# Attention and two MoE layers on one core: block 0 and block 1 scaled by pairs of heads, the third weight unit loaded and decoded sooner, other idle products

## The chip, the cores and the metric

The kernel runs on one core of a Trainium2 chip. Its engines are TensorE (PE, with PEld for its weight loads), VectorE (DVE), ScalarE (ACT), GpSimd (POOL) and SyncE (SP, which here only issues DMAs). The metric is the device time of one execution in microseconds; the median of three runs of the kernel before is 1569.9 us (1569.37 to 1571.35).

## The reference

```
kv  = k^T v per batch and head          (8 batches, 8 heads, 576 rows, head size 64)
out = q kv
x   = out / rms(out over a head) * g_norm            -> 4608 rows of 512
xn  = x / rms(x over 512) * rms_g
h   = silu(xn @ w_gate) * (xn @ w_val)                (512 x 1536 each)
x2  = h @ w_out                                       (1536 x 512)
y   = relu(x2 @ w_in)^2 @ w_out2                      (512 x 2048, 2048 x 512)
```

The reference's weights are float64; the kernel receives them as 64-bit words and makes pairs of fp32r numbers (a rounded high part and a low rest) of them on the chip. All products are three passes over such pairs.

## The kernel before, in words

The 4608 rows are nine blocks of 512. Stages take one or two blocks through a layer; the first stage is layer 1 for blocks 0 and 1. `x_stage` makes the gate and value products (line 831, tile `c`; 12 products for one result bank), `h_stage` the products after them.

**Units.** A unit is a slice of 256 columns of one weight matrix: `g0`, `v0`, `g1`, `v1`, `g2`, `v2` and so on for gate and value. In `prep_unit` it passes through these steps, in this order: `load` (SP, line 153, tile `wraw`, 1 MB), `bits_1` (ACT, line 161, `wps`), `bits_2` (ACT, line 165, `wpw`), `bits_3` and `bits_4` (DVE, lines 171 and 177, in `wpw`), `hi_0` (ACT, line 225, rounds to `ws`), `lo_0` (DVE, line 232, the rest to `ws`), `words_out` (SP, line 188, the decoded words to the DRAM tensor `wf_g` or `wf_v`), `put_0` (SP, line 240, `ws` to `wd_g`). A product on a unit's columns needs its `hi_0` for the first passes and its `lo_0` for the last. The tiles `wps` and `wpw` come from rings: `v2` decodes into the tile that held `g1`'s words, so its `bits_2` waits until the DMA `wf_g` of `g1` has landed. Each engine runs its instructions in the order written. A DMA that SP issues also waits for the one eight places before it.

**The order.** `prep_first` gives every step of every unit a number, and `steps_of` sorts them into a list; `prep_step` pops the next entry. Ahead of the first products the main program calls `prep_step` by hand; after that `tick`, called after each six products, runs what is due (`at`, `after`) and pops one entry.

**The head.** `keep(n)` issues n idle products of the identity (line 1251, tile `idle`). The head makes kv of batch 0 (line 458, `kvps`), copies it (line 500), makes the products with q for block 0 (`o_mm2`, line 537, `ops`), then kv of batch 1 with idle products between. For block 0 ACT squares `ops` (line 1271, `sq`), POOL multiplies by g_norm squared (line 572), DVE sums over heads (`att_sum`, line 586), makes the scale (`att_m`, `att_r`, lines 592 to 622) and scales (`att_y2`, line 639, `y`). Sixteen transposes (`x1_T`, line 646, `xps`) turn block 0; `x_hi` (ACT, line 668) and `x_lo` (DVE, line 672) round it to `xo`. Then `x_stage` begins with `g0`, `v0`, `g1`, `v1`, `g2`, `v2` on block 0 (24 products for each unit), while `o_events` does the same attention steps for block 1 (`att_c2`, line 565; squares, line 558; `att_half`, line 580; `att_y`, line 634) beside them, and turns block 1 between the products on `v2`.

The instruction buffers of an engine are filled by DMA too; the page lists the queue as "q8 instruction".

Of the kernel before, what the change touches and what calls it, by code (L numbers as in the profile page):

```python
# [11 lines left out]
F32 = mybir.dt.float32  # L12
# [37 lines left out]
def attn_moe_moe(  # L50
# [31 lines left out]
    tmp = ctx.enter_context(tc.tile_pool(name="t", bufs=8))  # L82
    psum = ctx.enter_context(tc.tile_pool(name="psum", bufs=1, space=bass.MemoryType.PSUM))
    ps_att = ctx.enter_context(tc.tile_pool(name="ps_att", bufs=1, space=bass.MemoryType.PSUM))
# [245 lines left out]
    def prep_first(units, raws):  # L330
# [3 lines left out]
        for n, (key, kind, base, room, places) in enumerate(units):  # L334
# [4 lines left out]
            for t, fn in steps:  # L339
                t += base + (late and t >= 3)  # L340
                events.append((t, n + 100 * (n == 1 and fn.__name__ in ("hi_0", "lo_0")), fn))
        return steps_of(events)

# [184 lines left out]

    def o_mm2(i, places=((ps_att, "A"), (ps_att, "B"))):
        ps = [pool.tile([128, 2, NP, D], F32, tag=tag, name="ops") for pool, tag in places]  # L530
        for c in range(2):
# [163 lines left out]
    def o_events(j, t, gap, first_t=0, direct=False):  # L695
# [22 lines left out]
        if not direct:  # L718
# [4 lines left out]
            return  # L723
        for c in range(NQ):
            at(u + 5 + c // 2, lambda c=c: att_y(j, c))
        for c in range(KC):
            v = first_t + c // 2
            place = ((ps_att, "A"), (ps_att, "B"), (psum, "b4"), (psum, "b5"))[c]
            at(v, lambda c=c, place=place: x1_T(j, c, *place))
            at(v + 1, lambda c=c: (x_hi(j, c), x_lo(j, c)))  # L730
# [61 lines left out]
    due = {}  # L792
    pace = {"prep": 0.0, "p": 0.0}

# [25 lines left out]

    banks = deque((4, 5, 0, 1, 2, 3))

# [32 lines left out]
    def x_stage(layer, blocks, early):  # L855
# [8 lines left out]
        for n, t in visits:  # L864
# [48 lines left out]
            if plain:  # L913
                bk = [banks.popleft() for _ in range(4)]
                fresh = ((0, 0), (0, 1), (1, 0)) if first[0] and n and t == 1 else PASSES
                w = {}
                for g, r in [(g, r) for g in range(2) for r in "12"] if first[0] else [(g, r) for r in "12" for g in range(2)]:
                    ps = bank(bk[2 * (r == "2") + g])
                    if not first[0] and g == 0:
                        w = {c: w_take(part(pair, r + c)) for c in "12"}  # L920
                    for c in "12":
# [263 lines left out]
    with tc.manual_schedule():  # L1185
# [40 lines left out]
        assert lo == len(l2_units)  # L1226
        prep_q.extend(preps[0])
# [12 lines left out]
        nc.gpsimd.tensor_tensor(out=gg_rg, in0=rg_sb, in1=gr_sb[:, D + KC:].to_broadcast([128, KC]), op=ALU.mult)  # L1240
        for place in *[(kvpool, "kv")] * 3, (rawp, "raw2_21"), (rawp, "raw1_11"):
            kv_load(*place)
        for _ in range(4):
            q_load()
        for _ in range(5):
            prep_step()
        idle = psum.tile([128, 512], F32, tag="b3", name="idle")

        def keep(n):
            for _ in range(n):  # L1250
                nc.tensor.matmul(idle[:, :128], lhsT=ident, rhs=ident, start=True, stop=True)  # L1251

        keep(14)
        kv_new(0, psum, "b4")
# [3 lines left out]
        kv_out(0)  # L1258
        for i in (0, 2):
            o_mm2(i, ((psum, f"b{i}"), (psum, f"b{i + 1}")))  # L1260
        idle = ps_att.tile([128, 512], F32, tag="A", name="idle")
        keep(16)
        kv_new(1, psum, "b5")
        for c in range(len(SC)):
            kv_whole(1, c)
            keep(2 if c < 4 else 0)
# [8 lines left out]
        for n in range(NQ):  # L1275
            att_sum(n, 0)
            if n:
                att_sum(n - 1, 1)
        att_sum(NQ - 1, 1)
        for _ in range(3):  # L1280
            prep_step()
        kv_out(1)
        keep(2)
# [6 lines left out]
        prep_step()  # L1290
# [6 lines left out]
        for _ in range(2):  # L1297
            prep_step()
        at(EARLY, lambda: fetch(3))
        o_events(1, 1, 3, 22, True)  # L1300

# [81 lines left out]
```

## Time and profile before

| what | value |
|---|---|
| median of three runs | 1569.9 us |
| the profiled execution, device time | 1570.27 us |
| its span | 1568.4 us |
| PE busy | 1555.3 us (99%) |
| DVE, ACT, POOL busy | 1184.2, 727.9, 63.8 us |
| mean granted TensorE clock | 1.00 |

The profiled execution is 0.37 us above the median. PE is busy nearly throughout, in part with idle products; what can change is how long it takes to reach the stretch in which it never waits. Rows of a timeline begin with the start and the duration in us; "x6" is a count of merged instructions, and the brackets hold the engine's idle time before and what ended it.

### The profile page before, as it was taken

The page shows a single profiled execution, that of the slowest core. Times are in us where ns is not written, and L with a number is a line of the kernel's source. Part 1 is how long each engine was busy: PE and PEld are TensorE (multiplying, and loading weights), DVE is VectorE, ACT ScalarE, POOL GpSimd, SP SyncE. Part 2 cuts the span into 40 slices and gives each one's busy share as a digit, 9 for nine tenths or more (in the row PEclk, how much of TensorE's full clock was granted, in tenths as well). Part 3 has the DMA queues.
Part 4 walks back from the last instruction along what each step waited for, and adds up shares of the span by engine and source line. Part 5 has one row for each costly group of instructions (what it writes and reads, how often), then busy time and mean ns, then how long its engine had stood idle before and what let it go on. Part 6 is the DMA issues. An engine that isn't in the chain of part 4 may idle for free.

```text
span 1568.4 us, 23092 instructions
## 1 busy us (share of the span) xinstructions
PE 1555.3 (99%) x8800; PEld 1298.5 (83%) x8800; DVE 1184.2 (76%) x1594; ACT 727.9 (46%) x983; POOL 63.8 (4%) x50
## 2 busy tenths in 40 slices
PE   8999999999999999999999999999999999999998
PEld 7788888888788888888888888888888888888898
DVE  5879884658587787987779888856876697568666
ACT  5556452254445555466546543522443244334433
POOL 2201010010000001000000000000000000000000
PEclk9999999999999999999999999999999999999999
DMA  9999989999988899799988996786678667766796
GB/s 358 373 390 401 337 285 337 382 339 357 391 289 260 288 331 336 238 338 351 395 315 267 392 335 217 247 249 191 196 248 246 194 197 252 237 194 207 228 407 238
DMA packets 174701, 463.98 MB, mean 296 GB/s; under 512 B 13824, under 2 KB 47616, under 8 KB 170240
## 3 DMA queue, kind: packets, MB, share of 16 engines
q1 hardware_dynamic: 174048, 462.25, 85.0%
q8 instruction: 70, 1.15, 0.3%
q10 hardware_dynamic: 544, 0.26, 0.1%
q14 instruction: 39, 0.32, 0.1%
HBM read 362.84 MB, written 99.61 MB: 295 GB/s over the span
## 4 chain that ended last, share of the span: by engine, by line
PE 93%; DMA 4%; DVE 1%; ACT 0%; issue 0%; SPq 0%; DVEq 0%; ACTq 0%
PE c L831 52%; PE a L1094 21%; PE e L1094 10%; PE d L1094 5%; PE acc L1061 2%; DMA wpl<-wf_v 1%; PE ops L537 1%; PE kvps L458 1%; DMA wf_g<-wpw 1%; DMA wd_g<-ws 1%; DMA kvraw<-in_kv_dram 1%; PE idle L1251 0%; DMA wt<-wd_g 0%; DVE ws L232 0%; DVE wpl L196 0%
## 5 line engine op out<-in xcount | busy, mean ns | idle before, releaser
L831 PE MATMUL c<-xo,wt 128*128 128x512 f32 (+1 forms) x3480 | 758.6, 379 | 1.1 <-ACT s L842 1.1
L831 PEld LDWEIGHTS c<-xo,wt 128*128 128x128 f32 x3480 | 629.5, 188 | 124.4 <-ACT s L842 1.5
L1094 PE MATMUL a<-ho,wt 128*128 128x512 f32 (+1 forms) x1536 | 334.1, 376 | 0.0
L739 ACT ACTIVATE ho<-hr 128x1024 fp32r<-128x1024 f32 (+1 forms) x230 | 230.9, 1006 | 201.1 <-PE a L1094 97.4
L740 DVE TENSOR_TENSOR ho<-hr,ho 128x1024 fp32r<-128x1024 f32 (+1 forms) x230 | 265.2, 1155 | 76.8 <-ACT ho L739 76.0
L1094 PEld LDWEIGHTS a<-ho,wt 128*128 128x128 f32 x1536 | 275.4, 188 | 52.4
L842 ACT ACTIVATE s<-c 128x512 f32<-128x512 f32 (+1 forms) x228 | 129.5, 573 | 176.7 <-PE c L831 175.4
L846 DVE TENSOR_TENSOR c<-c,s 128x512 f32<-128x512 f32 (+1 forms) x174 | 112.9, 649 | 80.8 <-PE c L831 73.5
L1094 PE MATMUL e<-ho,wt 128*128 128x512 f32 (+1 forms) x768 | 166.8, 376 | 0.0
L1094 PEld LDWEIGHTS e<-ho,wt 128*128 128x128 f32 x768 | 137.8, 188 | 26.2
L743 DVE TENSOR_TENSOR hr<-hr 128x1024 f32<-128x1024 f32 (+1 forms) x128 | 148.9, 1163 | 2.2
L831 PE MATMUL c<-xo,ws 128*128 128x512 f32 x576 | 134.4, 392 | 1.9 <-DVE ws L232 1.2
L831 PEld LDWEIGHTS c<-xo,ws 128*128 128x128 f32 x576 | 107.0, 188 | 25.6 <-DVE ws L232 2.1
L740 DVE TENSOR_TENSOR xo<-xr,xo 128x1024 fp32r<-128x1024 f32 (+1 forms) x58 | 66.8, 1157 | 40.3 <-ACT xo L739 40.1
L907 DVE TENSOR_TENSOR hr<-c,hr 128x512 f32<-128x512 f32 x108 | 76.0, 704 | 22.3 <-PE c L831 20.6
L1094 PE MATMUL d<-ho,wt 128*128 128x512 f32 (+1 forms) x384 | 85.0, 376 | 0.0
L1094 PEld LDWEIGHTS d<-ho,wt 128*128 128x128 f32 x384 | 68.9, 188 | 13.1
L853 DVE SCALAR_TENSOR_TENSOR hr<-c 128x512 f32<-128x512 f32 (+1 forms) x120 | 76.6, 638 | 4.0
L850 ACT ACTIVATE hr<-hr 128x512 f32<-128x512 f32 x54 | 34.1, 632 | 93.0 <-DVE hr L846 93.0
L902 ACT ACTIVATE r<-c 128x512 f32<-128x512 f32 (+1 forms) x40 | 22.1, 554 | 113.6 <-PE c L831 101.0
L572 POOL TENSOR_TENSOR sq<-sq,gg_sb 128x512 f32<-128x512 f32 x32 | 50.5, 1577 | 543.4 <-ACT sq L558 508.4
L232 DVE TENSOR_TENSOR ws<-wpl,ws 128x1024 fp32r<-128x1024 f32 (+1 forms) x44 | 49.7, 1129 | 26.5 <-ACT ws L225 26.3
(88 smaller groups left out, 988.6 us busy)
## 6 DMA issues: line engine op xcount, KB each, us to landing
wt<-wd_g SPq DMA_DIRECT2D x150, 512.0 KB, 6.6
wt<-wd_i SPq DMA_DIRECT2D x140, 512.0 KB, 5.0
wt<-wd_p SPq DMA_DIRECT2D x140, 512.0 KB, 4.6
wt<-wd_o SPq DMA_DIRECT2D x96, 512.0 KB, 5.5
wd_g<-ws SPq DMA_DIRECT2D x23, 1024.0 KB, 10.3
kvraw<-in_kv_dram SPq DMA_DIRECT2D x35, 512.0 KB, 8.0
wraw<-in_wo_dram SPq DMA_DIRECT2D x14, 1024.0 KB, 9.2
x2d<-o SPq DMA_DIRECT2D x36, 256.0 KB, 6.3
```

The lines of the kernel that those rows point to most:

```text
L232: nc.vector.tensor_tensor(out=t[:, :, 1, :], in0=quarters(st["sw"[1 - h]])[:, q], in1=t[:, :, 0, :].bitcast(F32), op=ALU.subtract)
L572: nc.gpsimd.tensor_tensor(out=heads(sg), in0=heads(sq), in1=gg_sb.rearrange("p (o d) -> p o d", o=1).to_broadcast([128, H, D]), op=ALU.mult)
L739: nc.scalar.activation(out=dst[:, 0], in_=src, func=AF.Copy)
L740: eng.tensor_tensor(out=dst[:, 1], in0=src, in1=dst[:, 0].bitcast(F32), op=ALU.subtract)
L743: eng.tensor_tensor(out=o, in0=x, in1=y, op=ALU.subtract)
L831: nc.tensor.matmul(ps, lhsT=w[:, a, kc * 128:(kc + 1) * 128], rhs=x[:, b, kc, :], start=(start and n == 0 and kc == 0), stop=(n == 2 and k ...
L842: nc.scalar.activation(out=t, in_=ps, func=AF.Copy)
L846: nc.vector.tensor_tensor(out=o, in0=ps, in1=t, op=ALU.add)
L850: nc.scalar.activation(out=hr, in_=c, func=AF.Silu)
L853: nc.vector.scalar_tensor_tensor(out=hr, in0=c, scalar=0.0, in1=c, op0=ALU.max, op1=ALU.mult)
L907: after(2, lambda: nc.vector.tensor_tensor(out=hr, in0=c, in1=hr, op=ALU.mult))
L1094: nc.tensor.matmul(ps, lhsT=w[e][:, a, d * 128:(d + 1) * 128], rhs=x[:, b, e, :], start=(i in (1, 2, 5) and q == 0 and e == 0 and a + b == 0),
```

## The change

It does five things. For block 0 the scaling goes by pairs of heads over all rows (`att_y4`, eight instructions of 128x256) and is interleaved with the turning: two pairs are scaled, turned and rounded, and the products of the first visit begin on that half of x; the other half follows after them. The results of `o_mm2` for block 0 lie in a pool of their own that is closed afterwards. `g1` is loaded ahead of the q tiles of block 1, and its steps and those of `v0` are called by name; units from `v1` on stand two places earlier in the order, and the first `tick` pops nothing. Block 1 is scaled in pairs too (`att_yp`). Of the idle products the first fourteen of 128 columns become twenty-eight of 64.

```diff
+    def att_y4(j, c, p, ps):
+        rr = r_t[j][:, :NS].rearrange("p (c a h o) -> p c a h o", a=NP, h=2, o=1)[:, c:c + 2, p]
+        y = y_t[j][:, c:c + 2, :].rearrange("p c (a h d) -> p a c h d", h=2, d=D)[:, p]
+        o = ps.rearrange("p h (c a d) -> p a c h d", a=NP, d=D)[:, p]
+        nc.vector.tensor_tensor(out=y, in0=o, in1=rr.to_broadcast([128, 2, 2, D]), op=ALU.mult)
+    def att_yp(j, p):
+        yh = y_t[j].rearrange("p c (a h d) -> p a c h d", h=2, d=D)[:, p]
+        rr = r_t[j][:, :NS].rearrange("p (c a h o) -> p a c h o", a=NP, h=2, o=1)[:, p]
+        nc.vector.tensor_tensor(out=yh, in0=yh, in1=rr.to_broadcast([128, NQ, 2, D]), op=ALU.mult)
...
-        for c in range(NQ):
-            at(u + 5 + c // 2, lambda c=c: att_y(j, c))
+        for p in range(NP):
+            at(u + 5 + p // 2, lambda p=p: att_yp(j, p))
...
-    pace = {"prep": 0.0, "p": 0.0}
+    pace = {"prep": 0.0, "p": -1.0}
...
+                if (n, t) == visits[0] and first[0]:
+                    lots[:2] = [(0, r, c) for c in "12" for r in "12"]
...
-            (key, "words", 4 * n + 3 * (n > 0), room if n % 3 < 2 else room_s, (at,))
+            (key, "words", 4 * n + 3 * (n > 0) - 2*(n>2), room if n % 3 < 2 else room_s, (at,))
...
+        do(g1, "load")
         for _ in range(4):
             q_load()
-        for _ in range(5):
-            prep_step()
+        do(g0, "bits_1", "bits_2", "bits_3", "bits_4", "hi_0", "lo_0")
...
-        keep(14)
+        keep(28, 64)
...
-        for n in (0, 2):
-            for h, ps in enumerate(o_ps.pop(n)):
-                att_y2(0, n, h, ps)
-        prep_step()
-        for c in range(KC):
-            x1_T(0, c, psum, f"b{c}")
-        for c in range(KC):
+        for c in range(2):
+            y_pair(c)
+            x1_T(0, c, ps_att, "AB"[c])
             x_hi(0, c)
-        for c in range(KC):
+        do(g1, "bits_1", "bits_2")
+        do(g2, "load")
+        for c in range(2):
             x_lo(0, c)
+        y_pair(2)
+        y_pair(3)
...
+        do(v0, "bits_3", "bits_4")
+        def rest():
+            for c in (2, 3):
+                x1_T(0, c, psum, f"b{c}")
+                x_hi(0, c)
+            for c in (2, 3):
+                x_lo(0, c)
+            do(v0, "hi_0", "lo_0")
+            do(g1, "bits_3", "bits_4")
+        at(2, rest)
```

On PE, at the end of the head, this stood before (`xps` are the transposes, `c` the first products):

```order
L1251 MATMUL idle_345<-ident_96 128x128 x2
L646 MATMUL xps_467<-ident_96,y_412 128x128 x4
L646 MATMUL xps_472<-ident_96,y_412 128x128 x4
L646 MATMUL xps_477<-ident_96,y_412 128x128 x4
L646 MATMUL xps_482<-ident_96,y_412 128x128 x4
L831 MATMUL c_505<-xo_487,ws_213 128x512 x6
L537 MATMUL ops_512<-kvb0_98,qt_199 64x64
```

And now, at the same place:

```order
L1294 MATMUL idle_218<-ident_96 128x128 x2
L680 MATMUL xps_478<-ident_96,y_430 128x128 x4
L680 MATMUL xps_487<-ident_96,y_430 128x128 x4
L865 MATMUL c_515<-xo_483,ws_215 128x512 x6
L865 MATMUL c_522<-xo_483,ws_215 128x512 x6
L680 MATMUL xps_529<-ident_96,y_430 128x128 x4
L680 MATMUL xps_536<-ident_96,y_430 128x128 x4
L558 MATMUL ops_549<-kvb0_98,qt_201 64x64
```

Eight transposes and six products have changed places; the q products of block 1 stand behind them as before.

On DVE, around the decoding of `g2` and `v2`, this stood before (`ws_747` is `g2`'s low part, `wpw_736` holds `v2`'s words, `ss` and `m` are the sums and means of block 1):

```order
L586 TENSOR_REDUCE ss1_558<-sq_680 128x8
L586 TENSOR_REDUCE ss1_558<-sq_720 128x8
L592 TENSOR_SCALAR m_757<-ss0_557 128x32
L593 RECIPROCAL ss0_557<-m_757 128x32
L594 TENSOR_TENSOR ss0_557<-ss0_557,ss1_558 128x32
L596 TENSOR_REDUCE m_757<-ss0_557 128x4
L597 TENSOR_SCALAR m_757<-m_757 128x4
L232 TENSOR_TENSOR ws_747<-wpw_683,ws_747 128x4x256
L171 SCALAR_TENSOR_TENSOR wpw_736<-wps_735,wpw_736 128x1024
L907 TENSOR_TENSOR hr_501<-c_738,hr_501 128x512
```

And now (`ws_748` is `g2`'s low part, `wpw_736` again holds `v2`'s words):

```order
L243 TENSOR_TENSOR ws_748<-wpw_644,ws_748 128x4x256
L182 SCALAR_TENSOR_TENSOR wpw_736<-wps_735,wpw_736 128x1024
L607 TENSOR_REDUCE ss0_594<-sq_758 128x8
L188 SCALAR_TENSOR_TENSOR wpw_736<-wps_735,wpw_736 128x1024
L607 TENSOR_REDUCE ss0_594<-sq_719 128x8
L607 TENSOR_REDUCE ss1_595<-sq_720 128x8
L941 TENSOR_TENSOR hr_511<-c_765,hr_511 128x512
L607 TENSOR_REDUCE ss1_595<-sq_759 128x8
L613 TENSOR_SCALAR m_798<-ss0_594 128x32
L614 RECIPROCAL ss0_594<-m_798 128x32
L615 TENSOR_TENSOR ss0_594<-ss0_594,ss1_595 128x32
L617 TENSOR_REDUCE m_798<-ss0_594 128x4
```

Block 1's last four sums and its means (`m`, five rows) stood ahead of `g2`'s low part and of `v2`'s `bits_3`; now one sum stands between `v2`'s `bits_3` and `bits_4`, and three sums and the means between `bits_4` and `v2`'s low part, which comes seven rows after the last one shown. The first five steps of the scale (`r`, `a`, `a`, `a`, `r`) stood between `bits_3` and `bits_4` and now stand behind `bits_4`; the last four stood ahead of the low part and now stand behind it. Of the two gate products `hr` in `v2`'s steps one is left there, behind `bits_4`.

On SP, from the last kv tile of batch 1 on, this stood before (`wraw_431` is `g1`'s load, `wraw_465` `v1`'s, `wraw_565` `g2`'s):

```order
L451 DMA kvraw_197<-in_kv_dram 64x1024
L507 DMA qt_199<-in_qt_dram 128x512
L507 DMA qt_201<-in_qt_dram 128x512
L507 DMA qt_203<-in_qt_dram 128x512
L507 DMA qt_205<-in_qt_dram 128x512
L153 DMA wraw_431<-in_wg_dram 128x2048
L188 DMA wf_g0_433<-wpw_208 128x1024
L240 DMA wd_g0_0_125<-ws_213 512x1x512
L153 DMA wraw_465<-in_wv_dram 128x2048
L153 DMA wraw_565<-in_wg_dram 128x2048
```

And now (`wraw_199` is `g1`'s load, `wraw_453` `v1`'s, `wraw_497` `g2`'s):

```order
L472 DMA kvraw_197<-in_kv_dram 64x1024
L164 DMA wraw_199<-in_wg_dram 128x2048
L528 DMA qt_201<-in_qt_dram 128x512
L528 DMA qt_203<-in_qt_dram 128x512
L528 DMA qt_205<-in_qt_dram 128x512
L528 DMA qt_207<-in_qt_dram 128x512
L164 DMA wraw_453<-in_wv_dram 128x2048
L199 DMA wf_g0_455<-wpw_210 128x1024
L251 DMA wd_g0_0_125<-ws_215 512x1x512
L164 DMA wraw_497<-in_wg_dram 128x2048
```

`g1`'s load has passed the four q tiles, and `v1`'s load the DMAs of `g0`'s words. From the next row to `g1`'s words (`wf_g1`, the 33rd DMA of the program) both queues hold the same transfers in the same order.

## Rows read from the trace of the kernel before

**Rows 1.** The page, part 1: busy time and share of each engine.
```profile
PE 1555.3 (99%) x8800; PEld 1298.5 (83%) x8800; DVE 1184.2 (76%) x1594; ACT 727.9 (46%) x983; POOL 63.8 (4%) x50
```
**Rows 2.** The chain of waits, 0 to 130 us: start, duration (us), what.
```profile
15.09 2.23 issue
...
17.89 3.77 PE idle L1251 x32
...
32.51 4.32 PE c L831 x18
...
42.10 13.32 DMA wf_g<-wpw
...
73.01 20.62 PE c L831 x90
```
**Rows 3.** The timeline of PE, 29 to 75 us.
```profile
29.71 1.71 PE L831 MATMUL c<-xo,ws 128*128 128x512 f32 x6
...
56.35 4.83 PE L831 MATMUL c<-xo,ws 128*128 128x512 f32 x20 [0.98 <-DVE ws L232]
61.82 1.19 PE L831 MATMUL c<-xo,ws 128*128 128x512 f32 x4 [0.64 <-ACT ws L225]
63.25 2.10 PE L831 MATMUL c<-xo,ws 128*128 128x512 f32 x8 [0.24 <-DVE ws L232]
...
68.44 3.03 PE L831 MATMUL c<-xo,ws 128*128 128x512 f32 x12
```
**Rows 4.** The timeline of PE, 400 to 426 us.
```profile
413.32 11.20 PE L831 MATMUL c<-xo,wt 128*128 128x512 f32 x48 [1.10 <-ACT s L842]
```
**Rows 5.** The timeline of DVE, 22 to 64 us.
```profile
25.61 2.48 DVE L639 TENSOR_TENSOR y<-ops,r 128x512 f32<-128x512 f32 x4
...
44.02 0.73 DVE L586 TENSOR_REDUCE ss<-sq 128x8 f32<-128x256 f32 x2
...
50.00 2.20 DVE L177 SCALAR_TENSOR_TENSOR wpw<-wps,wpw 128x1024 int32<-128x1024 int32 x1
52.12 1.92 DVE L586 TENSOR_REDUCE ss<-sq 128x8 f32<-128x512 f32 x4
53.96 0.17 DVE L592 TENSOR_SCALAR m<-ss 128x32 f32<-128x32 f32 x1
...
55.07 1.22 DVE L232 TENSOR_TENSOR ws<-wpw,ws 128x1024 fp32r<-128x1024 f32 x1
56.70 1.23 DVE L171 SCALAR_TENSOR_TENSOR wpw<-wps,wpw 128x1024 int32<-128x1024 int32 x1 [0.41 <-ACT wpw L165]
57.84 0.68 DVE L907 TENSOR_TENSOR hr<-c,hr 128x512 f32<-128x512 f32 x1
58.44 0.17 DVE L607 TENSOR_SCALAR r<-m 128x36 int32<-128x36 int32 x1
...
59.45 1.22 DVE L177 SCALAR_TENSOR_TENSOR wpw<-wps,wpw 128x1024 int32<-128x1024 int32 x1
...
61.98 1.22 DVE L232 TENSOR_TENSOR ws<-wpw,ws 128x1024 fp32r<-128x1024 f32 x1
```
**Rows 6.** The timeline of POOL, 15 to 60 us.
```profile
19.08 2.52 POOL L572 TENSOR_TENSOR y<-sq,gg_sb 128x512 f32<-128x512 f32 x2 [0.90 <-ACT sq L1271]
...
49.74 1.37 POOL L572 TENSOR_TENSOR sq<-sq,gg_sb 128x512 f32<-128x512 f32 x1 [2.00 <-ACT sq L558]
```
**Rows 7.** The timeline of SP, 0 to 80 us.
```profile
25.30 0.33 SPq L153 DMA_DIRECT2D wraw<-in_wv_dram  x1
```
**Rows 8.** Windows: PE, PEld, DVE, ACT, POOL busy, PE clock, DMA share, GB/s.
```profile
34.00:36.00 2.00, 2.00 (x11) 1.65 (x10) 2.00 (x3) 1.97 (x5) 0.00 (x0) 1.00 0.93 221
...
38.00:43.00 5.00, 5.00 (x82) 3.99 (x81) 3.02 (x2) 4.01 (x6) 4.87 (x5) 1.00 1.00 405
43.00:47.00 4.00, 4.00 (x19) 3.33 (x18) 4.00 (x7) 2.32 (x4) 3.92 (x4) 1.00 1.03 264
```
**Rows 9.** The DMA queues, 14.8 to 15.0 us: packets, MB, share of 16 engines.
```profile
q8 instruction: 1, 0.02, 31.8%
```

More of the change, by code (lines that the diff above doesn't have):

```diff
@@ L527, in fetch, with o_mm2 @@
                 fetches.popleft()()
-    def o_mm2(i, places=((ps_att, "A"), (ps_att, "B"))):
-        ps = [pool.tile([128, 2, NP, D], F32, tag=tag, name="ops") for pool, tag in places]
+    def o_mm2(i, places=None):
+        ps = places or [ps_att.tile([128, 2, NP, D], F32, tag=tag, name="ops") for tag in "AB"]
         for c in range(2):
@@ L819, in flush @@
             tick()
-    banks = deque((4, 5, 0, 1, 2, 3))
+    banks = deque((4, 0, 5, 1, 2, 3))
     def bank(n, name="c"):
@@ L916, in x_stage @@
                 w = {}
-                for g, r in [(g, r) for g in range(2) for r in "12"] if first[0] else [(g, r) for r in "12" for g in range(2)]:
-                    ps = bank(bk[2 * (r == "2") + g])
+                lots = [(g, r, "12") for r in "12" for g in range(2)]
+                if first[0]:
+                    lots = [(g, r, "12") for g in range(2) for r in "12"]
+                if (n, t) == visits[0] and first[0]:
+                    lots[:2] = [(0, r, c) for c in "12" for r in "12"]
+                into = {}
+                for g, r, cs in lots:
+                    if (g, r) not in into:
+                        into[g, r] = bank(bk[2 * (r == "2") + g])
+                    ps = into[g, r]
                     if not first[0] and g == 0:
                         w = {c: w_take(part(pair, r + c)) for c in "12"}
-                    for c in "12":
+                    for c in cs:
                         wt = w_direct(pair[g], *part(pair, r + c)[1:]) if first[0] else w[c][g]
@@ L1226, in attn_moe_moe @@
         assert lo == len(l2_units)
-        prep_q.extend(preps[0])
         nc.vector.memset(zero, 0.0)
@@ L1230, in attn_moe_moe @@
         nc.scalar.activation(out=zero, in_=zero, func=AF.Silu)
-        prep_step()
+        g0, v0, g1, v1, g2 = gv[:5]
+        soon = [step_of[k] for k in ((v0, "hi_0"), (v0, "lo_0"), (g1, "bits_3"), (g1, "bits_4"))]
+        do(g0, "load")
         for c in range(len(SC)):
@@ L1236, in attn_moe_moe @@
             q_load()
-        prep_step()
+        do(v0, "load")
         make_identity(nc, ident)
@@ L1258, in attn_moe_moe @@
         kv_out(0)
-        for i in (0, 2):
-            o_mm2(i, ((psum, f"b{i}"), (psum, f"b{i + 1}")))
-        idle = ps_att.tile([128, 512], F32, tag="A", name="idle")
+        ps_0 = ExitStack()
+        o_pool = ps_0.enter_context(tc.tile_pool(name="o_0", bufs=1, space=bass.MemoryType.PSUM))
+        o_0 = [o_pool.tile([128, 2, T], F32, tag=f"o{n}", name="ops") for n in range(2)]
+        for n in range(2):
+            o_mm2(2 * n, places=[o_0[n][:, h].rearrange("p (c a d) -> p c a d", c=2, d=D) for h in range(2)])
         keep(16)
@@ L1265, in attn_moe_moe @@
             kv_whole(1, c)
-            keep(2 if c < 4 else 0)
+            keep(2)
         sq_0 = ypool.tile([128, NQ, DM], F32, tag="xt", name="sq")
@@ L1274, in attn_moe_moe @@
                 att_sg(i)
[L1275 to L1281, printed above, removed]
+        do(v0, "bits_1", "bits_2")
+        att_sum(0, 0)
+        att_sum(1, 0)
+        att_sum(0, 1)
+        att_sum(2, 0)
+        att_sum(3, 0)
+        att_sum(1, 1)
+        att_sum(2, 1)
+        att_sum(3, 1)
+        do(v1, "load")
+        do(g0, "words_out", "put_0")
         kv_out(1)
-        keep(2)
         att_m(0)
@@ L1286, in attn_moe_moe, with y_pair @@
             att_r(0, n)
-        for n in (0, 2):
-            for h, ps in enumerate(o_ps.pop(n)):
-                att_y2(0, n, h, ps)
-        prep_step()
-        for c in range(KC):
-            x1_T(0, c, psum, f"b{c}")
-        for c in range(KC):
+        def y_pair(p):
+            for n in range(2):
+                att_y4(0, 2 * n, p, o_0[n])
+        for c in range(2):
+            y_pair(c)
+            x1_T(0, c, ps_att, "AB"[c])
             x_hi(0, c)
-        for c in range(KC):
+        do(g1, "bits_1", "bits_2")
+        do(g2, "load")
+        for c in range(2):
             x_lo(0, c)
-        for _ in range(2):
-            prep_step()
+        y_pair(2)
+        y_pair(3)
+        ps_0.close()
+        psum.open()
+        o_ps.clear()
+        do(v0, "bits_3", "bits_4")
[8 more added lines that the diff above has]
+        at(2, rest)
+        prep_q.extend(steps_of([e for e in preps[0] if e[2] not in made_first and e[2] not in soon]))
         at(EARLY, lambda: fetch(3))
-        o_events(1, 1, 3, 22, True)
+        o_events(1, 2, 3, 22, True)
         l2 = ExitStack()
```

27 lines of the change are left out of this document (20 added, 7 removed).

## The prediction

> **What bounds the kernel now.** I read the shares first: PE is busy for 1555.3 of 1568.4 us [rows 1], so only its few gaps, and idle or late work that counts as busy, can be won. The chain of waits, read next, tells where those are: idle products and an "issue" gap of 2.23 us in the head, then the DMA of `g1`'s words (13.32 us), and from 73.01 us on PE alone [rows 2]. PE's timeline gives the waits of the first stage one by one: 0.98, 0.64 and 0.24 us between 55 and 63.3 us, all on units `g2` and `v2` [rows 3]; behind that the one wait of size is 1.10 us at 413 us, on ACT [rows 4], which the change does not touch. So one number decides: when PE gets to block 1's first products, at 68.44 + 1.4 = 69.8 us (the row's first six products are still `v2`'s). All behind it is the same work on an engine that does not wait. The units behind `v2` come no later than before, and PE waited for none of them; so I cost their two earlier places, the banks and the places of the q products at nothing, since PE's own products hide them (were one of them late, a wait like the three of [rows 3] would come back, some 1 us).
>
> **The last wait before 69.8 us.** It is a chain of one DMA and two engines. `wf_g` of `g1` is issued at 42.10 us and lands at L = 55.42 [rows 2]. That frees the tile for `v2`'s `bits_2` (ACT, 1.23 us, the landing wait of the next row), and DVE goes on at 56.70 with `bits_3`, a gate product, five scale steps, `bits_4` at 59.45, another gate product, four steps, and the low part from 61.98 to 63.2, when PE goes on [rows 5, 3]. So the low part ends 7.8 us behind L, and block 1 begins 6.6 us behind that.
>
> **The change, part by part.**
>
> *Idle products.* Twenty-eight of 64 columns stand for fourteen of 128: the same columns. They lie ahead of the first kv tile, whose DMA PE waits for anyway, so their time is covered. But they are 28 products more in PE's instruction stream. The gap of 2.23 us [rows 2] begins just when the instruction queue moves a packet [rows 9], and no semaphore ends it; I read it as the refill of PE's instructions, which hangs on the count of instructions issued. Twenty-eight records earlier in the stream lies about one and a half kv tiles, 1.9 us, earlier: the q products of block 0 would end at 15.9 to 16.2 instead of 17.89, and the idle products and kv tiles of batch 1 behind them [rows 2], too. If the gap stays where it is, nothing is gained. I take the first.
>
> [...]
>
> *Scaling and turning by pairs.* POOL's sums waited 0.90 us for ACT's squares [rows 6], which come sooner with the q products, so the scaling begins at about 24.7 instead of 25.61 [rows 5]. A pair instruction (128x256) is not in the trace; a 128x512 one takes 2.48/4 = 0.62 us, a 128x256 sum 0.73/2 = 0.36 [rows 5]. I take 0.35, with 0.31 (half) and 0.42 as ends. The four that the first two turns need take 1.4 us (1.2 to 1.7) instead of 2.48. From the end of the scaling, 28.09, to the first product, 29.71 [rows 3], 1.62 us went to sixteen transposes and the rounding; now eight transposes are in the way, so between half of it and all, and I take 1.2: first product at 24.7 + 1.4 + 1.2 = 27.3. Beside it `g1` and `v0` are decoded in another order, and the gain shrinks on the way: on `v0`'s columns PE begins at some 35.2 instead of 36.83 (the end of the first 24 products, [rows 2]), an estimate from the DVE rows put in their new order: 1.5 us sooner, or 0.3 later if the refill stays. For the next units DVE and ACT are no longer in front of PE, so it comes to `v2` that much sooner, and without the waits of 0.98 and 0.64 [rows 3]: near 61.82 - 0.98 - 0.64 - 1.5 = 58.7. There it waits for the low part: this gain is a longer wait, not a shorter run.
>
> *`g1`'s load.* It passes four q tiles on SP, and `v1`'s load passes `g0`'s words and is issued at 21.5 instead of 25.30 [rows 7]. `v1`'s second step on ACT then ends 3 us sooner, and with the ring of eight `wf_g` of `g1` is issued at about 39.0 instead of 42.10. When it lands is the heart of it. With the same duration: 39.0 + 13.3 = 52.3. But ahead of it lie the same 32 transfers as before, and the DMA engines are full there: share 0.93 and 1.03 with 221 and 264 GB/s in the two thinnest windows [rows 8]. If the engines close those two thin stretches to the 405 GB/s of the one between them, (1 - 221/405) x 2 = 0.9 us and (1 - 264/405) x 4 = 1.4, L is 55.42 - 2.3 = 53.1. If nothing closes, it stays at 55.4. I take 53.1; the ends are 50.6 (below it DVE, not the DMA, is late) and 55.4.
>
> *`v2`'s chain on DVE.* This is what the change adds. Before, block 1's last sums, 1.92 us, and its means, 53.96 to 55.07, were done while DVE would have waited for L [rows 5]; now they are queued behind `v2`'s `bits_3`, and what waits for them is `v2`'s own low part, then PE. From the start of `bits_3`: `bits_3` 1.14, a sum 0.5 to 0.6, `bits_4` 1.14, two sums and one gate product and one sum 0.5 + 0.6 + 0.6 + 0.5, means 1.1, five scale steps 1.0, low part 1.2: 8.1 us, against 56.70 to 63.2 = 6.5 before. With ACT's 1.23 and the two handovers it ends L + 9.4. One step is dearer where POOL works beside it: `bits_4` of `g2` took 2.20 us beside POOL's last product against 1.22 alone [rows 5, 6]; POOL's last product now falls into this chain, so up to 0.7 more: L + 9.4 to L + 10.1. With L = 53.1: 62.5 to 63.2, against 63.2.
>
> *Behind it.* The second gate product and four scale steps, 0.6 + 0.9, now follow the low part, but the first turn needs only one instruction of the scaling (128x512, 0.62 by the row of 25.61 [rows 5]) where it needed four, 2.48. The transposes come between PE's products on `v2`, and block 1 begins 6.8 us behind the low part instead of 6.6.
>
> **The sum.** Block 1 begins at (62.5 to 63.2) + 6.8 = 69.3 to 70.0 instead of 69.8: between 0.5 us sooner and 0.2 later. The middle is 0.15 sooner on the profiled execution's 1570.27 us, which is 0.37 above the median of the runs shown, 1569.9. I forecast 1569.7. PE's busy time in the head falls, and its wait on `v2` grows by as much.
>
> **The rivals.**
>
> *The words land early.* If the DMA engines take `wf_g` as early as it is issued, L comes to 50.6 or less, and the chain begins when DVE is done with `g2`'s low part at 51.8 to 52.8. Then `v2`'s low part ends at about 60.5 and block 1 starts 2.4 to 2.6 us sooner: 1567.3. For it speaks that PE now reaches `v2` near 58.7 and can use it; against it the full DMA engines [rows 8].
>
> *The words land no sooner, and DVE's longer chain decides.* The rings are full, L = 55.4, and the chain of 9.4 to 10.1 us ends at 64.8 to 65.5: block 1 starts at 71.6 to 72.3, 1.8 to 2.5 us later: 1572.1. It decides as soon as L is over 53.8, where L + 9.4 plus 6.8 passes 69.8 + 0.2. For it: equal transfers ahead on full engines [rows 8] and 1.6 us more on DVE; against it that the thin windows have something to give.
>
> [...]
>
> *The change does not reach the chain.* The refill of PE's instructions falls into another stretch, after 30 us, where PE has no idle products to lose: a gap of 2.23 us [rows 2] is then paid if it lies behind `v2`, and PE had some 3 us to spare ahead of it. Cost 0 to 2.2: up to 1572.1. All three waits of [rows 3] gone and the head's gain paid out would be 1.86 + 2.4 = 4.3 us, 1565.6, the most that there is.
>
> **How the numbers follow.** Forecast 45 in 100, words early 24, words late 20, another place for the refill 5, everything paid out 6. A difference under 0.2%, 3.1 us, counts as none here, which is about what a measurement of this kernel can tell. The forecast's own range is 1569.0 to 1570.5. Words early gives 1566.5 to 1568.5, words late 1571 to 1573, so 1566.5 to 1572.7 holds over 8 in 10. Faster by over 3.1 us is the last case and a third of the early words (the low end passes 1566.8): 0.14. Slower by over 3.1 us, past 1573.0, takes late words with the dear `bits_4` and another loss, or the refill behind `v2` with late words: 0.09. The rest, 0.77, is no change that can be told.
>
> **What would show it.** In PE's timeline: the "issue" gap near 13 instead of 15.09, the first product near 27.3, one wait of some 3 to 4 us on `ws` near 58 to 63 in place of three small ones, block 1 at 69.3 to 70.0, and none behind. On SP `wf_g` of `g1` near 39.0, and its landing near 53.1: at or under 50.6 the first rival is right, near 55.4 the second. On DVE 8.1 to 8.8 us from `v2`'s `bits_3` to the end of its low part. A wait of PE behind 75 us that was not there before would make the whole argument wrong, as would an "issue" gap between the products.

## The result: 13 us slower, and the profile after

| kernel | median, us | runs |
|---|---|---|
| before | 1570.17 (1569.37 to 1571.35) | 6 |
| changed | 1583.26 (1581.21 to 1584.25) | 6 |

The ratio is 1.0079, with a 95% interval from 1.0069 to 1.0089: 11 to 14 us slower. The forecast was no change, 1569.7 us, with a range up to 1572.7. The profiled execution of the changed kernel took 1581.21 us (span 1579.4), 10.9 us over that of before. It is the fastest of the six; of the 13.1 us between the medians, some 2 lie in executions of which there is no trace.

Where the span grew is read from PE's timeline, by the same stations in both kernels. First the start of the kernel before (start, duration, then the instructions; "x28" counts records, two for each product):

```profile
1.36 5.31 PE L1251 MATMUL idle<-ident 128*128 128x128 f32 x28 [1.36 <-POOL ident masks.py:199]
6.88 0.69 PE L458 MATMUL kvps<-kvraw 128*64 128x64 f32 x16 [0.22 <-DMA kvraw<-in_kv_dram]
7.50 0.49 PE L1251 MATMUL idle<-ident 128*128 128x128 f32 x2
...
12.08 0.68 PE L458 MATMUL kvps<-kvraw 64*64 64x64 f32 x16
```

The same stretch of the changed kernel, and on to block 1:

```profile
1.36 12.21 PE L1294 MATMUL idle<-ident 128*128 128x64 f32 x56 [1.36 <-POOL ident masks.py:199]
13.49 1.12 PE L479 MATMUL kvps<-kvraw 128*64 128x64 f32 x16
14.55 0.80 PE L1294 MATMUL idle<-ident 128*128 128x128 f32 x2
...
19.87 0.49 PE L1294 MATMUL idle<-ident 128*128 128x128 f32 x2
20.29 0.68 PE L479 MATMUL kvps<-kvraw 64*64 64x64 f32 x16
21.46 2.10 PE L558 MATMUL ops<-kvb,qt 64*64 64x64 f32 x128 [0.48 <-ACT kvb L521]
...
35.11 3.39 PE L865 MATMUL c<-xo,ws 128*128 128x512 f32 x12 [0.30 <-ACT xo L702]
...
68.74 2.11 PE L865 MATMUL c<-xo,ws 128*128 128x512 f32 x8 [1.27 <-DVE ws L243]
...
74.20 3.03 PE L865 MATMUL c<-xo,ws 128*128 128x512 f32 x12
```

The idle products last 12.21 us instead of 5.31, so the first kv tile, whose data came at about 6.9 us in the kernel before, waits until 13.49 for PE itself. Its products then take 1.12 us a tile, where they took 0.69, and the idle products between the tiles 0.80 instead of 0.49: PE is on a lower level of its clock until about 19.9 us. (The column of the granted clock prints 1.00 here; the durations say otherwise, and the trace's first record of the granted clock, 1.00, stands at 19.80 us, in the kernel before at 5.40.) The "issue" gap of [rows 2] is gone from among the q products. The first product on block 0 comes at 35.11 instead of 29.71 [rows 3], and block 1 at 74.20 + 1.4 = 75.6 instead of 69.8: 5.8 us late. Where from is a question for the experiments.

Behind block 1, where the prediction had PE never wait, two rows have waits. From PE's timeline at 150 to 200 and 400 to 440 us of the changed kernel:

```profile
185.51 5.69 PE L1136 MATMUL a<-ho,wt 128*128 128x512 f32 x24 [3.56 <-DMA wt<-wd_o]
...
424.31 11.20 PE L865 MATMUL c<-xo,wt 128*128 128x512 f32 x48 [2.20 <-ACT s L876]
```

and the row of before at the first of these places:

```profile
176.00 5.60 PE L1094 MATMUL a<-ho,wt 128*128 128x512 f32 x24
```

The first products with `w_out` wait 3.56 us for their weights, which had been there before; the wait of [rows 4] has doubled. 5.8 + 3.56 + 1.10 = 10.5 of the 11.0 us between the spans. The last of the three can't be laid to the change: in the other profiles, of both kernels, that wait is anything from none to 1.30 us long. The prediction had named a new wait of PE behind 75 us as the sign that its whole argument is wrong, and there is one.

### The profile page after: what moved, and what is told of

It is laid out like the page before. It is cut to its first block, busy times and chain, and to the rows that moved or that the text cites. A ratio compares the mean times of both kernels' runs of the same rounds, so it can differ in the third digit from the quotient of the medians.

```text
span 1579.4 us, 23155 instructions
## 1 busy us (share of the span) xinstructions
PE 1565.0 (99%) x8828; PEld 1307.3 (83%) x8828; DVE 1185.8 (75%) x1598; ACT 726.9 (46%) x983; POOL 66.3 (4%) x50
## 4 chain that ended last, share of the span: by engine, by line
PE 86%; DMA 4%; DVE 2%; ACT 1%; issue 0%; SPq 0%; DVEq 0%; ACTq 0%
PE c L865 46%; PE a L1136 21%; PE e L1136 10%; PE d L1136 5%; PE acc L1103 2%; DMA wpl<-wf_v 1%; DMA wraw<-in_wo_dram 1%; PE ops L558 1%; DMA wd_g<-ws 1%; DVE ws L243 1%; PE kvps L479 0%; DMA wt<-wd_o 0%; DVE wpw L182 0%; DVE wpw L188 0%; DVE wps L207 0%
## 5 line engine op out<-in xcount | busy, mean ns | idle before, releaser
L1136 PEld LDWEIGHTS d<-ho,wt 128*128 128x128 f32 x384 | 68.9, 188 | 13.1
L243 DVE TENSOR_TENSOR ws<-wpl,ws 128x1024 fp32r<-128x1024 f32 (+1 forms) x44 | 49.7, 1129 | 27.5 <-ACT ws L236 27.3
## 6 DMA issues: line engine op xcount, KB each, us to landing
wd_g<-ws SPq DMA_DIRECT2D x23, 1024.0 KB, 11.1
```

The source lines that it names most:

```text
L243: nc.vector.tensor_tensor(out=t[:, :, 1, :], in0=quarters(st["sw"[1 - h]])[:, q], in1=t[:, :, 0, :].bitcast(F32), op=ALU.subtract)
L1136: nc.tensor.matmul(ps, lhsT=w[e][:, a, d * 128:(d + 1) * 128], rhs=x[:, b, e, :], start=(i in (1, 2, 5) and q == 0 and e == 0 and a + b == 0),
```

## The experiments

Two questions: are the idle products the cause of the late head, or do they only fill time that other parts of the change lost; and what makes the weights of `w_out` late, the late head or the order of the units? All ratios are against the kernel before, run beside the kernel.

| kernel | median, us | before, us | ratio, 95% |
|---|---|---|---|
| before, 28 idle products of 64 | 1577.65 | 1570.02 | 1.0032 to 1.0065 |
| changed, 14 idle of 128 | 1577.17 | 1570.02 | 1.0024 to 1.0054 |
| changed, 14 idle of 64 | 1576.89 | 1570.02 | 1.0025 to 1.0053 |
| changed, 28 idle of 128 | 1574.10 | 1570.02 | 1.0017 to 1.0036 |
| changed, 14 idle of 128, old places of the units | 1573.63 | 1569.64 | 1.0014 to 1.0032 |
| changed, 14 idle of 128, old first tick | 1577.36 | 1569.64 | 1.0029 to 1.0059 |
| changed, 14 idle of 128, both old | 1571.56 | 1569.64 | 0.9996 to 1.0015 |
| before, new places of the units | 1574.64 | 1569.64 | 1.0021 to 1.0040 |
| before, 28 idle of 64 with weights of 64 | 1570.78 | 1570.25 | 0.9995 to 1.0014 |
| changed, 14 idle of 128, only v1, g2, v2 moved | 1569.75 | 1570.25 | 0.9987 to 1.0006 |
| before, only v1, g2, v2 moved | 1570.62 | 1570.25 | 0.9994 to 1.0013 |
| before, g1's load ahead of the q tiles | 1571.22 | 1570.25 | 0.9997 to 1.0016 |
| changed, only v1, g2, v2 moved | 1578.46 | 1570.36 | 1.0030 to 1.0061 |
| changed, idle weights of 64, only v1, g2, v2 moved | 1569.14 | 1570.36 | 0.9986 to 1.0003 |

### The idle products

**The kernel before with twenty-eight idle products of 64 columns.**

```diff
-        keep(14)
+        keep(28, 64)
```

> The kernel before, with nothing changed but its first fourteen idle products of 128 columns, which become twenty-eight of 64. Theory A (an idle product of 64 columns takes as long as one of 128, about 0.21 us a record, and TensorE stays at its lower clock meanwhile): the idle stretch takes 12 us instead of 5.3, the kv products of batch 0 take 1.1 us a tile instead of 0.69, the gap of 2.23 us at 15 us is gone, block 1 starts near 75.5 instead of 69.8, and the time is 1575 to 1577 us. Theory B (the head is late for what the other parts of the change do, scaling by pairs and g1's load; the idle products only fill the time): 1570 us, within 1 us. Theory C (the late wait of 3.56 us at 185 us follows from the later head): as A, with a wait of 3 to 4 us near 185 too, 1579 to 1581 us.

Theory A holds, B falls: this edit alone costs 7.6 us, 0.65 us over the top of what was expected. Its rows at the start are those of the changed kernel (12.21 us for 56 records, tiles of 1.12 us). The first products with `w_out` come 6.4 us later than in the kernel before, without a wait, so C falls too:

```profile
182.42 5.61 PE L1094 MATMUL a<-ho,wt 128*128 128x512 f32 x24
```

**The changed kernel with fourteen of 128, fourteen of 64 and twenty-eight of 128.**

```diff
-        keep(28, 64)
+        keep(14)
```

The two others have `keep(14, 64)` and `keep(28)` there.

> The changed kernel with fourteen idle products of 128 columns again. Theory A: the idle stretch takes 5.3 us, the head is as early as before, block 1 starts at 69.3 to 70 us. With the late waits (3.56 at 185 us, 2.20 at 424 us) still there, since they come from the new places of the units, 1574 to 1576 us; if they come from the late head (Theory C), 1569 to 1571 us. Theory B: 1580 us or more, block 1 at 75 us.

> The changed kernel with fourteen idle products of 64 columns (half of its columns, as many products as before). Theory A: 28 records at 0.21 us, 6 us; TensorE is still at its lower clock when the first kv tile comes at 7 us, whose products take 1.1 us a tile, so that batch 0's kv ends 2 to 3 us later than with 128 columns and the time lies between the kernel with fourteen of 128 and the changed one, 2 to 3 us over the former. If only the count matters and not the clock: as fourteen of 128, within 1 us.

> The changed kernel with twenty-eight idle products of 128 columns (twice the columns, the new count). Theory A: the first 17 records at 0.21 us, then the clock rises and the other 39 take 0.12 to 0.16 us: 8.5 to 10 us, and the kv tiles behind take 0.69 us: batch 0's kv ends 2 to 3 us later than with fourteen, but 5 us sooner than in the changed kernel with 64 columns, though twice as many columns pass. If the price goes by columns, it is the slowest of the four, over the changed kernel's 1583 us.

With fourteen of 128, block 1 starts at 68.6 us, 7.0 sooner than in the changed kernel and 1.2 sooner than in the kernel before; the wait for `w_out`'s weights does not go, it grows to 6.22 us, and the clock falls in it. So the wait does not come from the late head, as theory C had it, and 7.2 us of the loss are left. Three views of this kernel: block 1, the wait, and the windows around it (busy time of PE, granted clock, DMA share, GB/s).

```profile
67.22 3.02 PE L865 MATMUL c<-xo,ws 128*128 128x512 f32 x12
...
181.16 8.10 PE L1136 MATMUL a<-ho,wt 128*128 128x512 f32 x24 [6.22 <-DMA wt<-wd_o]
```

```profile
176.00:178.00 2.00, 0.00 (x0) 1.00 1.02 321
...
180.00:182.00 2.00, 0.84 (x2) 0.50 1.09 371
182.00:184.00 2.00, 2.00 (x6) 0.50 0.91 209
...
190.00:194.00 4.00, 4.00 (x19) 1.00 1.07 390
```

Behind this wait PE runs on its lower level (0.50) until about 186 us: 24 records take 8.10 us instead of 5.60. So this wait cost more than itself. In the changed kernel's own profile the wait of 3.56 us had no such fall behind it (5.69 us); its slower executions, up to 1584.25 us, show a mean clock of 0.998 to 0.999.

The other two settle what the price of an idle product hangs on. The first line is of fourteen products of 64 columns, the rest of twenty-eight of 128:

```profile
1.36 6.24 PE L1294 MATMUL idle<-ident 128*128 128x64 f32 x28 [1.36 <-POOL ident masks.py:199]
```

```profile
1.36 9.39 PE L1294 MATMUL idle<-ident 128*128 128x128 f32 x56 [1.36 <-POOL ident masks.py:199]
10.68 0.69 PE L479 MATMUL kvps<-kvraw 128*64 128x64 f32 x16
...
15.97 1.39 PE L558 MATMUL ops<-kvb,qt 64*64 64x64 f32 x79 [0.48 <-ACT kvb L521]
17.56 0.97 PE L558 MATMUL ops<-kvb,qt 64*64 64x64 f32 x49 [0.20 <-issue]
```

Twenty-eight products of 128 columns take 9.39 us where twenty-eight of 64 took 12.21, because the clock rises during the products of 128 (at 7.4 us of the span) and not during those of 64. In the traces the records start 0.213 us apart at the lower level, with 64 and with 128 columns alike, and 0.112 apart once the clock has risen. Fourteen of 64 missed their expected total: kv of batch 0 did end 1.8 us later than with fourteen of 128, but the "issue" gap (1.62 us there) was no longer seen, and the head came out within 0.2 us. The last two rows bear on the refill: the gap stands behind 79 q records here and behind 107 with half as many idle products. The difference, 28, is the number of records put ahead (fourteen products of two records each).

**The kernel before with twenty-eight idle products of 64 columns, their weights 64 wide too.** The edit is shown against the kernel of the first experiment.

```diff
-    nc.tensor.matmul(idle[:, :w], lhsT=ident, rhs=ident[:, :w], start=True, stop=True)
+    nc.tensor.matmul(idle[:w, :w], lhsT=ident[:, :w], rhs=ident[:, :w], start=True, stop=True)
```

> The kernel before with twenty-eight idle products of 64 columns, as in the run where only that was changed (12.21 us for the 56 records, 1577.7 us), but the weights of an idle product are 64 columns wide too (the later idle products of 128 columns stay). Theory G (a short product's price is the loading of its 128 columns of weights): 0.11 us a record, 6 us, and the head is late by 1 to 3 us instead of 6 (1571 to 1574 us). Theory H (a record costs some 0.21 us at the lower clock whatever its columns): 12 us again, 1577 us.

Theory G holds, and the head is not even late by the 1 to 3 us that were expected:

```profile
1.36 5.50 PE L1251 MATMUL idle<-ident 128*64 128x64 f32 x56 [1.36 <-POOL ident masks.py:199]
6.91 0.69 PE L458 MATMUL kvps<-kvraw 128*64 128x64 f32 x16
```

The same number of products over the same columns, with half the weights to load, end before the first tile comes, the clock has risen by then (at 5.9 us), and the time is that of the kernel before. The clock is not what makes the difference in price: still at the lower level, the records start 0.107 us apart here and 0.213 us apart with 128 columns of weights. Of the price of an idle product of 64 columns, the 128 columns of weights are the part that counts.

### The places of the units

**The changed kernel with fourteen idle products of 128, and the old places, the old first tick, or both.**

```diff
-            (key, "words", 4 * n + 3 * (n > 0) - 2*(n>2), room if n % 3 < 2 else room_s, (at,))
+            (key, "words", 4 * n + 3 * (n > 0), room if n % 3 < 2 else room_s, (at,))
```

```diff
-    pace = {"prep": 0.0, "p": -1.0}
+    pace = {"prep": 0.0, "p": 0.0}
```

> The changed kernel with fourteen idle products of 128 columns (its head is as early as before; it waits 6.22 us near 175 us for the weights of w_out, and measured 1577.2 us), and now the units from v1 on at their old places in the order. Theory D (the two earlier places order the decoding so that w_out's units come late): the wait near 175 us is gone or under 1 us, and the time is 1568 to 1571 us. Theory E (the later start of the ticks' count delays all decoding): the wait stays, 1574 to 1578 us. Theory F (neither; the steps called by name and the half of block 0 that follows delay it): the same as E.

> As the kernel with fourteen idle products of 128 columns, with the units at their new places, but the first tick pops an entry of the order again. Theory E: the wait for w_out's weights is gone, 1568 to 1571 us. Theories D and F: it stays, 1574 to 1578 us.

> As the kernel with fourteen idle products of 128 columns, with the old places of the units and the old first tick. Theories D and E: no wait near 175 us, 1568 to 1571 us, at best 1.2 us under the kernel before (block 1 starts 1.2 us sooner, at 68.6). Theory F: the wait of several us stays, 1574 to 1578 us.

With the old places there is no wait for `w_out`'s weights; with the old first tick alone it stays, 2.78 us. So D holds against E and F. The total with the old places alone, 1573.6, is over what was expected: `v2`'s low part is then late, and PE waits 2.79 us for it at 62 us. With all units moved, PE had no such wait (the kernel with fourteen of 128, which is otherwise the same). With both old places and the old first tick the wait for `w_out`'s weights is gone too, and 1571.6 us can't be told from the kernel before; PE still waits 1.91 us for `v2`'s low part in its profile.

**The kernel before with the new places alone.** The edit is the change's own `- 2*(n>2)`.

> The kernel before, with the units from v1 on two places earlier in the order and nothing else changed. Theory D: a wait of 2 to 6 us for w_out's weights appears near 176 us, and the time is 1572 to 1577 us. Theories E and F: no such wait, 1570 us, within 1 us.

D again: the wait appears, and the cost is 5.0 us between the medians (the profiled execution is the fastest of ten, 1571.5 us, and shows less). Block 1 comes 1.3 us sooner, and then `w_out`'s weights are waited for. PE's rows first, then the row of SP with the four DMAs of `w_out`'s words ahead of it, and the row of SP that answers to it in the kernel before:

```profile
67.17 3.04 PE L831 MATMUL c<-xo,ws 128*128 128x512 f32 x12
...
178.60 5.68 PE L1094 MATMUL a<-ho,wt 128*128 128x512 f32 x24 [3.68 <-DMA wt<-wd_o]
```

```profile
157.56 14.36 SPq L240 DMA_DIRECT2D wd_o<-ws  x4
```

```profile
152.82 14.47 SPq L240 DMA_DIRECT2D wd_o<-ws  x4
```

The words go out 4.7 us later. With PE 1.3 us sooner and a wait of 3.7, PE had about 4.7 + 1.3 - 3.7 = 2.3 us to spare in the kernel before.

The clock goes with a part of the spread of its ten executions at most: the fastest (1571.5 us) shows a mean clock of 1.000 and two of the slow ones (1576.1 and 1576.3) 0.996, but 1572.6 and 1576.5 us both came with 0.998.

Why earlier places make `w_out` later is in the rules of `prep_step`, worked out by counting at which tick each entry is popped. The entry at the head of the list can be held, and then nothing behind it goes: `bits_3` of `g3` until the 24th tick (`BEGIN`), a `w_out` unit's `bits_1` until six ticks after its load (`LAND`).

| step of the first `w_out` unit | tick, old places | tick, new places |
|---|---|---|
| load (number 30) | 18 | 24 |
| `bits_1` | 26 | 30 |
| last DMA, `put_1` | 41 | 43 |

`g3`'s held step has number 31 at its old place, behind the load, and 29 at its new one, ahead of it. The load is popped behind the hold, `bits_1` is held until six ticks after that, and the entries behind stand 2 to 3 ticks later through most of the list. A tick is six products, 1.37 us (20.62 us for 90, [rows 2]): 2.7 to 4.1 us, more than the 2.3 us to spare. Against PE's products the words are 4.7 + 1.3 = 6.0 us later; what makes up the rest was not followed.

**Only `v1`, `g2` and `v2` moved, in both kernels.** This keeps `g3` behind the load. The edit is shown for the changed kernel; the kernel before gets the same line.

```diff
-            (key, "words", 4 * n + 3 * (n > 0) - 2*(n>2), room if n % 3 < 2 else room_s, (at,))
+            (key, "words", 4 * n + 3 * (n > 0) - 2 * (2 < n < 6), room if n % 3 < 2 else room_s, (at,))
```

> The changed kernel with fourteen idle products of 128 columns, and of the units only v1, g2 and v2 two places earlier; g3 and v3 are back at 21 + 3 + 3 and so behind the load of w_out's first unit. Theory D2 (g3's bits_3, which is held until the 24th tick, went ahead of that load, so that its bits_1 is held to the 30th tick instead of the 26th and all later steps stand 2 to 3 ticks later): no wait near 175 us for w_out's weights, block 1 near 68.6 us or up to 1 us later, 1568 to 1570.5 us. Rival D1 (the earlier places of v1, g2 and v2 do it): the wait of 2 to 6 us stays, 1573 to 1578 us.

> The kernel before with v1, g2 and v2 alone two places earlier. Theory D2: the head of the kernel with all units moved (block 1 at 68.6 us instead of 69.8) without its wait of 3.68 us: 1568 to 1570 us. Rival D1: the wait stays, 1572 to 1577 us.

D2 holds in both: no wait for `w_out`'s weights, and no difference from the kernel before that can be told. In the changed kernel, the profiled execution lost its gain in the head, since a fall of the clock (0.50 at 18 to 20 us, behind the "issue" gap of 1.93 us) stretched the sixteen idle products from 3.84 to 5.33 us; in the kernel before with this edit the same happened (5.46 us):

```profile
18.07 5.33 PE L1294 MATMUL idle<-ident 128*128 128x128 f32 x32
```

### One part alone, and all of the rest

**The kernel before with `g1`'s load ahead of the q tiles.**

```diff
+        g1_load = next(fns for fns in prep_q if fns[0].__name__ == "load")
+        g1_load.pop()()
         for _ in range(4):
             q_load()
```

> The kernel before with g1's load alone ahead of the q tiles of block 1. If the bytes ahead of g1's words set when they land (the second rival of the prediction): no change within 1 us, 1569 to 1571 us, or 0.5 us later where the q tiles of block 1 now land later. If an earlier issue is an earlier landing: block 1 starts 1 to 2.5 us sooner, 1567 to 1569 us.

No gain: block 1 starts at 69.3 instead of 69.8 us in its profile, and the interval holds no change. The waits on the low parts of `g2` and `v2` are there as before (0.95 and 0.24 us). The edit does not bring `wf_g` forward (issued at 42.06 us, before at 42.10), so it cannot tell what an earlier issue is worth. In this profile the words land at 53.0 us, 2.4 us sooner than before, and it helps little: DVE goes straight from `g2`'s low part to `v2`'s `bits_3` at 56.13, so DVE and not the DMA is in front.

**The changed kernel with one of the two faults mended, and with both.**

> The changed kernel with g3 and v3 alone put back to their old places in the order; the idle products stay twenty-eight of 64 columns. If the two causes add up (idle products +7.6 us in the kernel before, places of the units +5.0 us there): the wait near 185 us is gone, block 1 still starts near 75.6 us, and 1575 to 1578 us. If the wait near 185 us came from the late head and not from the order: it stays, over 1580 us.

> The changed kernel with both edits mended: the weights of the twenty-eight idle products are 64 columns wide too, and g3 and v3 stand at their old places. If scaling by pairs, g1's earlier load and the sooner refill of PE's instructions together bring what the prediction summed, 0 to 0.5 us, plus the earlier end of batch 0's q products: block 1 between 68 and 70 us, 1567.5 to 1570.5 us. If the first rival of the prediction holds without the two faults (words early, DVE in front): block 1 near 67.5 us and 1566 to 1568 us.

With the order alone mended the wait for `w_out`'s weights is gone and 8.1 us of loss are left, about what the idle products cost in the kernel before (7.6). Block 1 starts at 78.0 us in its profile, not near 75.6: the clock rose only at 26.0 us there (19.8 in the changed kernel), and the q products of block 0 took 3.69 us instead of 2.10:

```profile
20.62 1.12 PE L479 MATMUL kvps<-kvraw 64*64 64x64 f32 x16
22.22 3.69 PE L558 MATMUL ops<-kvb,qt 64*64 64x64 f32 x128 [0.48 <-ACT kvb L521]
...
76.62 3.02 PE L865 MATMUL c<-xo,ws 128*128 128x512 f32 x12
```

The four executions lie between 1574.6 and 1580.3 us; that the clock's rise makes this spread is likely, and not shown. By themselves the two edits cost 7.6 and 5.0 us, 12.6 together, and the change cost 13.1: within the intervals they add up, and nothing of size is left over. With both mended block 1 comes at 67.05 + 1.4 = 68.5 us and no wait is left between the units:

```profile
67.05 3.03 PE L865 MATMUL c<-xo,ws 128*128 128x512 f32 x12
```

Its median is 1.2 us under that of the kernel before, its interval 0.9986 to 1.0003: between 2.2 us faster and 0.5 slower. This is the best of the kernels run, and not shown to beat the kernel before. Nor is its earlier block 1 shown to come from pairs or from `g1`'s load: the kernel before with the new places alone has block 1 at 68.6, and with nothing but other idle products (weights of 64) at 67.39 + 1.4 = 68.8 us, so about 1 us of it is within what one profile differs from another.

## Why the prediction was wrong, step by step

**Idle products: the step that failed.** "Twenty-eight of 64 columns stand for fourteen of 128: the same columns [...] so their time is covered." It priced a product by the columns that pass. The runs show 0.213 us a record at the lower level with 64 and with 128 columns, as long as the weights have 128; with weights of 64 it is 0.107, and the stretch fits. And it took the clock's rise for granted: it came 4.2 to 7.6 us into the span with columns of 128, and in the changed kernel at 19.8, some 6 us after the last product of 64; those kept PE going without a pause for 12.21 us. The first idle records beside later ones were in the trace of before (5.31 us for 28; 3.77 for 32 [rows 2]), and were not used. The forecast named what lay ahead of the first tile as cover without pricing the cover: about 5.5 us, against 12.21.

**The places of the units: the second step that failed.** "The units behind `v2` come no later than before, and PE waited for none of them; so I cost their two earlier places [...] at nothing [...]". The units `g3` and `v3` were called earlier by their numbers; that an earlier step can be a held one, with others queued behind it, was not followed. The cost if wrong was put at 1 us; alone it is 5.0 us.

**The refill: right, but for a word.** "28 products more" are fourteen products more, of 28 records. The gap moves by the count of instructions, behind 79 records instead of 107. In the two kernels with idle weights of 64 the instruction queue moves its packet at 13.15 and 12.91 us, not at 14.87 as before (1.9 us sooner was forecast), and no gap is left. In the changed kernel the packet moves at 18.39, and PE's q products begin only at 21.46, so it never waits for it. Less was gained than the forecast took: with weights of 64 the q products end at 16.9 to 17.0 us, not at 15.9 to 16.2, since PE then waits 0.65 to 0.90 us for a q tile.

**The first product on block 0: a third step that failed, though the sum did not hang on it.** "[...] first product at 24.7 + 1.4 + 1.2 = 27.3." In the kernel with both faults mended it comes at 29.14, before at 29.71. First DVE's pairs, then PE at the end of the head:

```profile
25.21 1.42 DVE L667 TENSOR_TENSOR y<-ops,r 128x256 f32<-128x256 f32 x4
```

```profile
26.91 0.71 PE L1294 MATMUL idle<-ident 128*128 128x128 f32 x4
27.73 1.06 PE L680 MATMUL xps<-ident,y 128*128 128x128 f32 x8
29.14 3.39 PE L865 MATMUL c<-xo,ws 128*128 128x512 f32 x12 [0.34 <-ACT xo L702]
32.37 1.03 PE L680 MATMUL xps<-ident,y 128*128 128x128 f32 x8
```

The scaling is done at 26.63, but PE is with batch 1's kv and its idle products until 27.62, and the transposes stand behind them. That part of PE's order is missing in the sum. The other half of the turning, 1.03 us, now lies behind the first products, so PE is not early at `v2` and has no wait of 3 to 4 us there. Instead the three waits of [rows 3] are gone: 0.57 + 1.86 - 1.03 = 1.4 us, by which block 1 is earlier.

**Pairs: right in size.** Four pair instructions take 1.42 us (predicted 1.4), in DVE's timeline of the changed kernel:

```profile
32.90 1.42 DVE L667 TENSOR_TENSOR y<-ops,r 128x256 f32<-128x256 f32 x4
...
59.56 1.64 DVE L182 SCALAR_TENSOR_TENSOR wpw<-wps,wpw 128x1024 int32<-128x1024 int32 x1 [0.74 <-ACT wpw L176]
...
61.72 1.72 DVE L188 SCALAR_TENSOR_TENSOR wpw<-wps,wpw 128x1024 int32<-128x1024 int32 x1
...
67.47 1.22 DVE L243 TENSOR_TENSOR ws<-wpw,ws 128x1024 fp32r<-128x1024 f32 x1
```

**`v2`'s chain: right without the two faults, over the range with them.** In the changed kernel it takes 9.1 us from the start of `bits_3` (59.56) to the end of the low part (68.7), predicted 8.1 to 8.8; the same chain of before took 6.5 [rows 5]. `bits_3` and `bits_4` are both dear here (1.64 and 1.72 us). The terms that the prediction lists add up to 8.3, not 8.1. In the kernel with both faults mended the chain takes 8.4 us, from 53.12 to 61.5:

```profile
53.12 1.39 DVE L182 SCALAR_TENSOR_TENSOR wpw<-wps,wpw 128x1024 int32<-128x1024 int32 x1 [0.29 <-ACT wpw L176]
...
60.31 1.22 DVE L243 TENSOR_TENSOR ws<-wpw,ws 128x1024 fp32r<-128x1024 f32 x1
```

**The landing of `g1`'s words: between the forecast and the first rival.** In the kernel with both faults mended `wf_g` is issued at 40.71 and lands 11.1 us later, at 51.8 us, where the prediction took 39.0 and 53.1 with bounds of 50.6 and 55.4. From there the sum holds: the low part ends 9.7 us behind the landing (predicted 9.4 to 10.1), and block 1 begins 6.9 behind that (predicted 6.8). PE comes to it just then and waits for no unit, and block 1 starts 1.4 us sooner than before, where 0.5 sooner to 0.2 later was predicted. The earlier issue is that of the new places and not of `g1`'s load: with the places alone `wf_g` is issued at 39.36 us and lands at 51.6. From issue to landing it takes 10.9 to 12.6 us in all other profiles, and 13.3 only in the one that the prediction was read from.

**The rivals.** None was it. "The words land no sooner" is against the rows: issued at 39.4 to 40.9 us they land at 51.6 to 52.3, not at 55.4. "Everything paid out" had it right that all three waits of [rows 3] can go, and no rival had a cost in the idle products or behind block 1. The range, 1566.5 to 1572.7, holds the change without its two faults (1569.14), though the head gained otherwise than was summed up.

## What to carry to other kernels

Price a small product by the columns of its weights too, and not by its own columns alone (0.213 us a record with 128 columns of weights and 0.107 with 64 here), at the clock level of its place, and put the sum against the cover in us, before calling idle work free; work that is meant to bring the clock up must be seen to do so in the rows (here the clock rose 4.2 to 7.6 us into the span with idle products of 128 columns, and at 19.8 in the changed kernel). Where an order has entries that can be held, an earlier number is not an earlier step: follow which entries stand behind the held one, and compare the shift with what the consumer has to spare. Read the waits behind the changed stage too, for a cost there was as large as one in the stage.

## What the runs showed that was not expected

One wait of PE cost twice: in and behind the 6.22 us wait of the changed kernel with fourteen idle products of 128 the granted clock stood at 0.50 for 6.8 us (179.5 to 186.3), which made 24 records 2.5 us longer. Seven of the profiles have such falls, all but one of the falls at waits of 1.67 to 6.22 us; other waits, of 1.62 to 3.68 us and in seven profiles, had none. What decides it stays open. The column of the granted clock showed 1.00 in the first 20 us of the changed kernel, where the durations are those of the lower level.
